# Attention with an MLP between: seven score runs per 16 key blocks, and the value sums read out by VectorE

## The chip, the cores and the metric

The kernel runs on one core of a Trainium2 chip. The metric is the device time of one execution in microseconds (us), the median over several runs; less is better. The core has a matrix engine (TensorE, "PE" in the profile, its weight loads "PEld"), VectorE ("DVE"), ScalarE ("ACT"), GpSimd ("POOL") and SyncE ("SP"), which here only issues DMA transfers. Each engine works through its own queue in order; semaphores make one engine wait for another.

## The reference

Attention and an MLP are computed from the same normalised input and added to the input (S = 2048 tokens, D = 640, 32 heads of 20, F = 1536):

```python
xn = layernorm(x)
qkv = (xn @ wqkv).reshape(B, S, 3, 32, 20).transpose(2, 0, 3, 1, 4)
p = softmax((q @ k.T) * 20 ** -0.5)
a = (p @ v).transpose(0, 2, 1, 3).reshape(B, S, 640) @ wo
y = layernorm(xn)
m = gelu(y @ w1 + b1, approximate=True) @ w2 + b2
out = x + a + m
```

## The kernel before

A first stage (up to about 232 us) normalises the input and computes queries, keys and values, and splits the weights into pairs of f16 numbers. The stage that the change touches is the attention loop, from there to about 1306 us. After it comes the rest of the projection by `wo` and the output.

**The attention loop.** The heads go in 16 pairs g, the queries in halves hf of 1024 tokens and quarters cc of 512; the keys in NKB = 16 blocks kb of 128. `ORDER` lists the pairs and halves. For each (g, hf, cc), that is 64 times, the 16 key blocks are gone through; the text calls one such pass a period.

- `scores` (L578): for one key block, four entries on TensorE (two weight loads and two matmuls, one for each head of the pair) write a tile `s` of two PSUM banks, from a pool of three such tiles (`psS`). ScalarE takes the exp of it into an SBUF tile `p` (128 x 1024, L586), from a pool `pt`.
- `rest` (L593): for half of the key blocks (`SPLIT`: the first two of each four) VectorE computes `low`, what the upper 16 bits of each p leave over, in f16 (L598). There are four such buffers.
- `pv` (L603): the products with the values for four key blocks, 16 matmul calls on 32-column parts of the array (eight with the upper halves, four with `low`, four in f32), summed in one PSUM bank `o`, whose pool `psO` has one buffer. The bank collects all 16 blocks of a period. After the last four, ScalarE copies it into `ev` (L636), one half of a tile that holds two periods; when both halves are there, `unload` (L642) writes them to DRAM with two transfers to `lpart` (the sums of p) and four to `opart`, on SP's queue, or on ScalarE's for the last entry of `ORDER`.
- `finish` (L666): when some head pairs are complete, their sums are loaded again, checked, inverted, spread over the rows, and multiplied in by VectorE (L725 to L731), step by step.

**The MLP between.** `mlp` (L829) is a generator over chunks of 256 tokens. For each chunk there are six tiles of `layer1` (30 matmuls `pu` of 256 columns in one PSUM bank) and four of `layer2` for the chunk before (36 matmuls `py` of 320 columns). They share one PSUM bank, `psM`. It yields an estimated cost in us after three `pu` or two `py` matmuls. When a `layer1` tile ends, `gelu` (L735) is begun: its VectorE operations (L740, L741; then L744, L745), a tanh on ScalarE (L748), and three more on VectorE (L750 to L752). A `yield` in it means that it goes on at the next `tick`; `tick()` moves every such side job on by one step. The end of a `layer2` tile is one VectorE operation (L757). `load_chunk` (L769) loads a chunk's input and its row of factors `r2f`.

**The order written out by hand** is the loop at L933. For every four key blocks: scores of two blocks; a tick; `rest` of the first block; a part of the MLP; scores of two blocks; a tick; `rest` of the others; and `pv` of the four blocks before. The MLP part takes steps while the credit, which grows by `rate` = 1.235 for each four blocks, is above zero, up to `CHUNK` = 1.75 in one part, and stops where a tile ends (`over`). So a period has eight score runs, four MLP parts and four value runs on TensorE.

Of the kernel before, what the change touches and what calls it, by code (L numbers as in the profile page):

```python
# [7 lines left out]
F32 = mybir.dt.float32  # L8
# [8 lines left out]
P = 128  # L17
# [15 lines left out]
CHUNK = 1.75  # L33
# [9 lines left out]
def mha_mlp_kernel(tc, x, wqkv, wo, w1, b1, w2, b2, out):  # L43
# [4 lines left out]
    with (  # L48
# [463 lines left out]
        with ExitStack() as scope:  # L512
# [4 lines left out]
            ptp = pool(name="pt", bufs=2 * GRP - 1)  # L517
# [83 lines left out]
            evs = {}  # L601

            def pv(units):  # L603
# [29 lines left out]
                if last:  # L633
                    if cc == 0:
                        evs[g, hf] = m1.tile([P, 2, 512], F32, tag="ev", name="ev")
                    nc.scalar.activation(evs[g, hf][:, cc], pv.o, AF.Copy)  # L636
                    if cc == 1:
                        unload(g, hf, evs.pop((g, hf)))
# [5 lines left out]
            def unload(g, hf, ev):  # L644
                cols = slice(hf * 1024, (hf + 1) * 1024)
                for p in range(2):
                    dma(g, hf)(lpart[p, hf, 2 * g : 2 * g + 2, :].rearrange("a (c t) -> a c t", c=2),
                                      ev[PAD + DH + VW * p :: 64])
                    for a in range(2):
                        q0, r = 64 * a + PAD + VW * p, (2 * g + a) * DH  # L650
                        dma(g, hf)(opart[p, r : r + DH, cols].rearrange("d (c t) -> d c t", c=2),
                                          ev[q0 : q0 + DH])
# [82 lines left out]
            def gelu(ps, r2f, hT, f):  # L735
# [11 lines left out]
                yield  # L747
# [18 lines left out]
            xs, hTs = {}, {}  # L766
            over = [False]

            def load_chunk(mc):  # L769
                t0 = mc * MC  # L770
                xnt = m2.tile([P, KD, 2, MC], F16, tag="xnt", name="xm")
                r2f = m2.tile([P, MC], F32, tag="r2f", name="r2f")
                nc.sync.dma_start(xnt, xscr[:, :, :, t0 : t0 + MC])
                nc.sync.dma_start(r2f, rscr[None, t0 : t0 + MC].to_broadcast([P, MC]))
                xs[mc] = xnt, r2f

            def layer1(mc, f):
                xnt, r2f = xs[mc]
# [3 lines left out]
                for i in range(2):  # L782
                    n = 0
                    fo_ = (f + i) % 4 * P
                    for k in range(KD):
                        for a, b in PASS:
                            nc.tensor.matmul(ps[:, i], w1v[:, k, (f + i) // 4, a, fo_ : fo_ + P], xnt[:, k, b, :],  # L787
                                             start=(n == 0), stop=(n == 3 * KD - 1))
                            n += 1
                            if n % 3 == 0:  # L790
                                if i == 1 and n == 15:
                                    begin(gelu(ps, r2f, hTs[mc], f))
# [36 lines left out]
            def mlp():  # L829
                load_chunk(0)  # L830
                load_chunk(1)
# [95 lines left out]
            with tc.manual_schedule():  # L927
                fill = chain()
                credit = 0.0 - next(fill)
                rate = 1.235  # L930
                groups = [(g, hf, cc, kb) for g, hf in ORDER for cc in range(2) for kb in range(0, NKB, GRP)]
                prev = None
                for g, hf, cc, kb0 in groups:  # L933
                    units = []
                    for kb in range(kb0, kb0 + GRP):
                        units.append([g, hf, cc, kb, scores(g, hf, cc, kb)])
                        if kb % 2 == 0:
                            continue
                        tick()
                        if kb % GRP == 1:  # L940

                            rest(units[0])
                            credit += rate
                            spent, over[0] = 0.0, False
                            while credit > 0 and spent < CHUNK and not over[0]:
                                cost = next(fill)
                                if cost is None:
                                    credit = 0.0  # L950
                                    break
                                credit -= cost
                                spent += cost
                        else:
                            for u in units[1:]:
                                rest(u)
                            if prev:
                                pv(prev)
                    prev = units
                    if cc == 0 and kb0 == 0 and (g, hf) != ORDER[-1]:  # L960
                        n = ORDER[ORDER.index((g, hf)) + 1]
                        sides.append(load_stack(*n, *([stacks[g, hf][1]] if n[0] == g else [])))
# [15 lines left out]
                pv(prev)  # L978
# [104 lines left out]
```

## Time and profile before

| | us |
|---|---|
| median of 3 runs | 1384.39 (1383.7 to 1385.21) |
| the profiled execution | 1385.2 |
| its span from first to last instruction | 1383.5 |
| TensorE busy | 1350.8 (98% of the span) |
| ScalarE busy | 1126.2 (81%) |
| VectorE busy | 1061.7 (77%) |

Busy times are sums over the whole span, and the stages have different limits, so the attention loop is looked at by itself. A row of the groups gives the line, the engine, the operation, the tile written and the tiles read, the count, then busy time and mean duration (ns), then the engine's idle time just before with what ended it. A row of the waits gives who waited for whom, the total in us, how often, and the longest. A row of the timeline gives the start in us from the span's start, the time that a merged group took, the engine, the line and the operation, the count, and in brackets the idle time before it with what ended it. A row of a source line gives the count, then shortest, median and longest duration in ns, and the first and last start. PE busy time counts matmuls that wait in the array too, so starts of following runs tell more than durations.

### The profile page before, as it was taken

The numbers are of one execution on the slowest core, as the hardware profiler recorded it, in microseconds if no ns is written. First come the engines' busy times: TensorE is split into PE (matmuls) and PEld (weight loads), VectorE is DVE, ScalarE is ACT, GpSimd is POOL, SyncE is SP. The second block draws the span as 40 slices with busy tenths as digits, with TensorE's granted clock in tenths as the row PEclk, the third lists the DMA queues.
The fourth block names the chain that finished last, engine by engine and source line by source line (L and its number), as shares of the span: only waits on it lengthen the run. The fifth ranks groups of instructions, "written<-read, shape, count | busy, mean of one in ns | idle before, by whom it ended". The sixth has DMA issues, their size and how long they took to land.

```text
span 1383.5 us, 29113 instructions
## 1 busy us (share of the span) xinstructions
PE 1350.8 (98%) x11711; PEld 600.9 (43%) x11711; DVE 1061.7 (77%) x1425; ACT 1126.2 (81%) x1282; POOL 32.9 (2%) x75
## 2 busy tenths in 40 slices
PE   9999999999999999999999999999999999999998
PEld 6555555443333343433343333343334334333375
DVE  6648743899778977889887789877988897888642
ACT  5644323999999999999999999999999999999700
POOL 2000000000000000000000000000000000000000
PEclk9999999999999999999999999999999999999999
DMA  9853413012124231213221123212124322341375
GB/s 265 243 175 109 108 52 110 16 32 64 41 55 111 67 88 34 69 52 102 71 77 33 47 75 103 76 47 58 44 64 113 98 56 70 85 153 59 98 235 179
DMA packets 92320, 125.68 MB, mean 91 GB/s; under 512 B 16905, under 2 KB 58569, under 8 KB 92178
## 3 DMA queue, kind: packets, MB, share of 16 engines
q1 hardware_dynamic: 89218, 117.14, 28.3%
q0 software_dynamic: 2304, 5.24, 2.3%
q8 instruction: 94, 1.54, 0.5%
q10 hardware_dynamic: 656, 1.36, 0.3%
q14 instruction: 48, 0.39, 0.1%
HBM read 80.84 MB, written 42.86 MB: 89 GB/s over the span
## 4 chain that ended last, share of the span: by engine, by line
PE 59%; DVE 11%; ACT 5%; DMA 3%; issue 2%; SPq 1%; DVEq 0%; ACTq 0%
PE o L615 23%; PE s L584 14%; PE py L819 9%; PE pu L787 8%; DVE low L598 5%; PE z L896 5%; ACT p L586 4%; DMA oscr<-oa 1%; DVE u L740 1%; DMA oa<-opart 1%; DVE u L741 1%; DVE w L744 1%; DVE w L745 1%; DVE hT L752 1%; DVE u L750 1%
## 5 line engine op out<-in xcount | busy, mean ns | idle before, releaser
L586 ACT ACTIVATE p<-s 128x1024 f32<-128x1024 f32 x1024 | 973.6, 1042 | 52.4 <-PE s L584 46.2
L598 DVE TENSOR_TENSOR low<-p 128x1024 f16<-128x1024 f32 x512 | 608.8, 1219 | 165.0 <-ACT p L586 164.9
L615 PE MATMUL o<-p,vfull 128*32 128x512 bf16 (+1 forms) x4096 | 433.7, 494 | 0.0
L584 PE MATMUL s<-qs,ks 61*128 61x512 f16 x2048 | 317.7, 382 | 8.7 <-ACT p L586 7.2
L584 PEld LDWEIGHTS <-ks 61*128 61x128 f16 x2048 | 63.9, 94 | 296.4 <-issue 294.2
L787 PE MATMUL pu<-xm,w1t 128*128 128x256 f16 x1440 | 179.2, 274 | 4.1 <-DVE u L740 3.6
L819 PE MATMUL py<-w2t,hT 128*128 128x320 f16 x1152 | 178.6, 301 | 1.7 <-DVE xb L757 1.7
L787 PEld LDWEIGHTS <-w1t 128*128 128x128 f16 x1440 | 130.9, 98 | 71.2 <-issue 57.6
L819 PEld LDWEIGHTS <-hT 128*128 128x128 f16 x1152 | 102.5, 98 | 89.5 <-issue 55.2
L286 PE MATMUL qkp<-xnt,wv 128*128 128x512 f16 x600 | 132.3, 380 | 0.0
L615 PEld LDWEIGHTS <-vfull 128*32 128x32 f16 x3072 | 61.5, 95 | 146.2 <-issue 115.4
L615 PE MATMUL o<-low,vfull 128*32 128x512 f16 x1024 | 107.3, 379 | 6.6 <-DVE low L598 6.4
L300 ACT ACTIVATE qkhl<-qkp,qks 128x1024 f16<-128x1024 f32 (+1 forms) x24 | 23.3, 971 | 84.1 <-PE qkp L286 66.2
L286 PEld LDWEIGHTS <-wv 128*128 128x128 f16 x600 | 58.2, 98 | 67.8
L615 PEld LDWEIGHTS o<-p,vfull 128*32 128x32 f32 x2048 | 63.1, 109 | 50.6 <-issue 0.5
L349 PE MATMUL vp<-wv,xnt 128*128 128x320 f16 x480 | 66.6, 300 | 0.0
L896 PE MATMUL z<-w1t,ot 128*128 128x320 f16 x480 | 65.8, 300 | 0.0
L896 PEld LDWEIGHTS <-ot 128*128 128x128 f16 x480 | 46.7, 98 | 19.8 <-issue 1.7
L349 PEld LDWEIGHTS <-xnt 128*128 128x128 f16 x480 | 46.5, 98 | 18.2
L301 DVE SCALAR_TENSOR_TENSOR qkhl<-qkp,qks,qkhl 128x1024 f16<-128x1024 f32 (+1 forms) x24 | 26.5, 1104 | 34.3 <-ACT qkhl L300 34.3
L857 DVE SCALAR_TENSOR_TENSOR acc<-z,sc,acc 128x320 f32<-128x320 f32 x32 | 17.6, 550 | 45.1 <-PE z L896 42.9
L636 ACT ACTIVATE ev<-o 128x512 f32<-128x512 f32 x64 | 39.4, 615 | 3.3 <-PE o L615 3.3
(168 smaller groups left out, 685.7 us busy)
## 6 DMA issues: line engine op xcount, KB each, us to landing
qkscr<-qkhl SPq DMA_DIRECT2D x40, 256.0 KB
opart<-ev SPq DMA_DIRECT2D x124, 80.0 KB
ks<-qkscr SPq DMA_DIRECT2D x120, 80.0 KB
qs<-qkscr SPq DMA_DIRECT2D x192, 40.0 KB
oa<-opart SPq DMA_DIRECT2D x32, 240.0 KB
xt<-in_A_x_dram SPq DMA_DIRECT2D x16, 320.0 KB
xscr<-xnt SPq DMA_DIRECT2D x4, 1280.0 KB
xm<-xscr SPq DMA_DIRECT2D x8, 640.0 KB
```

The source lines that it names most:

```text
L286: nc.tensor.matmul(ps[:, i, :], wv[:, k, q, a, mm * P : (mm + 1) * P], xnts[c][:, k, b, :], start=(k + n == 0), stop=(k == KD - 1 and n == 2))
L300: nc.scalar.activation(hl[:, 0, i0:i1], ps[:, i0:i1], AF.Copy, scale=a)
L301: nc.vector.scalar_tensor_tensor(hl[:, 1, i0:i1], ps[:, i0:i1], a, hl[:, 0, i0:i1], ALU.mult, ALU.subtract)
L349: nc.tensor.matmul(ps[:, hf, :320], xnts[c][:, k, a, j * P : (j + 1) * P], wv[:, k, 2, b, hf * 320 : (hf + 1) * 320], start=(n == 0), stop ...
L584: nc.tensor.matmul(ps[:, a, :], ks[64 * a : 64 * a + 61, kb * P : (kb + 1) * P], qs[64 * a : 64 * a + 61, cc * 512 : (cc + 1) * 512], star ...
L586: nc.scalar.activation(pt, ps, AF.Exp, scale=QS)
L598: nc.vector.tensor_sub(low, pt, upper(pt))
L615: nc.tensor.matmul(pv.o[32 * q : 32 * q + 32, :], src[:, v0 - PAD * (1 - q % 2) :][:, :32], t, start=q not in pv.begun, stop=last, skip_gr ...
L636: nc.scalar.activation(evs[g, hf][:, cc], pv.o, AF.Copy)
L787: nc.tensor.matmul(ps[:, i], w1v[:, k, (f + i) // 4, a, fo_ : fo_ + P], xnt[:, k, b, :], start=(n == 0), stop=(n == 3 * KD - 1))
L819: nc.tensor.matmul(ps[:, :320], hTs[mc][:, f, a, j * P : (j + 1) * P], w2v[:, f, b, hf * 320 : (hf + 1) * 320], start=(n == 0), stop=(n == ...
L896: nc.tensor.matmul(ps[:, :320], ot[:, k, a, j * P : (j + 1) * P], wov[:, k, b, h * 320 : (h + 1) * 320], start=(n == 0), stop=(n == 3 * KD ...
```

## The change

The order of a period is written anew. Scores run in seven runs, up to blocks 3, 5, 7, 9, 12, 14 and 16. After each there is a tick, then `rest` of all new blocks, and then one piece of other work: an MLP part after 3, 7 and 14, and the value products of the last period's blocks 12 to 15 after 5, and of this period's blocks 0 to 3, 4 to 7 and 8 to 11 after 9, 12 and 16. `rate` is 1.647 for each of the three parts (1.235 x 4 = 4.94 for a period before), `CHUNK` is 2.0. The pool of p tiles has eight buffers for seven. VectorE copies the value sums out of PSUM, into a buffer of 512 tokens (one buffer), and `unload` writes each 512 tokens at once, with the same six transfers of half the size. `gelu` has one `yield` less. The factors `r2f` have one buffer for two and are loaded by `load_factors`, when the last `layer1` tile of the chunk before has ended, ahead of `load_chunk` for the chunk after.

```diff
-CHUNK = 1.75
+CHUNK = 2.0
-            ptp = pool(name="pt", bufs=2 * GRP - 1)
+            ptp = pool(name="pt", bufs=2 * GRP)
...
                 if last:
-                    if cc == 0:
-                        evs[g, hf] = m1.tile([P, 2, 512], F32, tag="ev", name="ev")
-                    nc.scalar.activation(evs[g, hf][:, cc], pv.o, AF.Copy)
-                    if cc == 1:
-                        unload(g, hf, evs.pop((g, hf)))
+                    ev = m1.tile([P, 512], F32, tag="ev", name="ev")
+                    nc.vector.tensor_copy(ev, pv.o)
+                    unload(g, hf, cc, ev)
...
-            def unload(g, hf, ev):
-                cols = slice(hf * 1024, (hf + 1) * 1024)
+            def unload(g, hf, cc, ev):
+                c0 = cc * 512
                 for p in range(2):
-                    dma(g, hf)(lpart[p, hf, 2 * g : 2 * g + 2, :].rearrange("a (c t) -> a c t", c=2),
-                                      ev[PAD + DH + VW * p :: 64])
+                    dma(g, hf)(lpart[p, hf, 2 * g : 2 * g + 2, c0 : c0 + 512], ev[PAD + DH + VW * p :: 64])
                     for a in range(2):
                         q0, r = 64 * a + PAD + VW * p, (2 * g + a) * DH
-                        dma(g, hf)(opart[p, r : r + DH, cols].rearrange("d (c t) -> d c t", c=2),
-                                          ev[q0 : q0 + DH])
-                if g + 1 in ENDS:
+                        dma(g, hf)(opart[p, r : r + DH, hf * 1024 + c0 : hf * 1024 + c0 + 512], ev[q0 : q0 + DH])
+                if cc == 1 and g + 1 in ENDS:
...
                 nc.vector.scalar_tensor_tensor(w, w, 1.0 / 0.044715, u, ALU.add, ALU.mult)
                 yield
-                yield
                 nc.scalar.activation(w, w, AF.Tanh, scale=0.7978845608028654 * 0.044715)
...
+            def load_factors(mc):
+                r2f = m1.tile([P, MC], F32, tag="r2f", name="r2f")
+                nc.sync.dma_start(r2f, rscr[None, mc * MC : (mc + 1) * MC].to_broadcast([P, MC]))
+                fs[mc] = r2f
...
                 if f == KF - 2:
+                    if mc + 1 < NMC:
+                        load_factors(mc + 1)
                     if mc + 2 < NMC:
                         load_chunk(mc + 2)
...
-                rate = 1.235
-                groups = [(g, hf, cc, kb) for g, hf in ORDER for cc in range(2) for kb in range(0, NKB, GRP)]
...
+                rate = 1.647
+                after = {3: "mlp", 5: -GRP, 7: "mlp", 9: 0, 12: GRP, 14: "mlp", 16: 2 * GRP}
+                prev, units, new = None, [], []
+                for g, hf in ORDER:
+                    for cc in range(2):
+                        prev, units = units, []
+                        for kb in range(NKB):
+                            units.append([g, hf, cc, kb, scores(g, hf, cc, kb)])
+                            new.append(units[-1])
+                            work = after.get(kb + 1)
+                            if work is None:
+                                continue
+                            tick()
+                            for u in new:
+                                rest(u)
+                            new.clear()
+                            if work == "mlp":
+                                credit += rate
+                                spent, over[0] = 0.0, False
+                                while credit > 0 and spent < CHUNK and not over[0]:
+                                    cost = next(fill)
...
+                            elif work >= 0:
+                                pv(units[work : work + GRP])
+                                units[work : work + GRP] = [None] * GRP
+                            elif prev:
+                                pv(prev[work:])
+                                prev = None
+                                del u
+                            if cc == 0 and work == -GRP and (g, hf) != ORDER[-1]:
+                                n = ORDER[ORDER.index((g, hf)) + 1]
+                                sides.append(load_stack(*n, *([stacks[g, hf][1]] if n[0] == g else [])))
```

More of the change, by code (lines that the diff above doesn't have):

```diff
@@ L791, in layer1 @@
                                 if i == 1 and n == 15:
-                                    begin(gelu(ps, r2f, hTs[mc], f))
+                                    begin(gelu(ps, fs[mc], hTs[mc], f))
                                     over[0] = True
@@ L929, in mha_mlp_kernel @@
                 credit = 0.0 - next(fill)
-                rate = 1.235
-                groups = [(g, hf, cc, kb) for g, hf in ORDER for cc in range(2) for kb in range(0, NKB, GRP)]
[L932 to L955, printed above, removed]
-                                rest(u)
[L957 to L962, printed above, removed]
```

17 lines of the change are left out of this document (10 added, 7 removed).

## The prediction

> **What bounds the kernel now.** I read the page's first and fourth parts, then the busy time of the stage with the attention loop (253 to 1309 us), then TensorE's waits in it, then the timeline of single groups. The page, and the windows' row (busy us and instructions of PE, PEld, DVE, ACT, POOL, then clock, DMA):
>
> ```profile
> span 1383.5 us, 29113 instructions
> PE 59%; DVE 11%; ACT 5%; DMA 3%; issue 2%; SPq 1%; DVEq 0%; ACTq 0%
> 253.00:1309.00 1056.00, 1036.06 (x9618) 413.67 (x9618) 887.23 (x1058) 1002.65 (x1126) 15.92 (x18) 1.00 0.25 69
> PE o L615 <- DVE low L598: 6.4, 11, 1.5
> PE s L584 <- ACT p L586: 5.7, 21, 0.5
> PE pu L787 <- DVE u L740: 3.6, 4, 2.0
> PE py L819 <- DVE xb L757: 1.7, 2, 1.3
> ```
>
> TensorE is busy 98% of the stage, ScalarE 95%, VectorE 84%; the chain of waits is mostly TensorE's. TensorE waits little, and not mainly for ScalarE. What one period (16 key blocks, 512 tokens) takes is the distance between two read-outs of the value sums: the source's row gives the first start, the timeline's the 63rd.
>
> ```profile
> L636 ACT ACTIVATE ev<-o x64: 597/601/750, 253.6 to 1309.7; 128x512 f32<-128x512 f32 x64
> 1295.36 0.60 ACT L636 ACTIVATE ev<-o 128x512 f32<-128x512 f32 x1
> ```
>
> (1295.36 - 253.6) / 62 = 16.80 us. Of this TensorE's own work, from starts in the timeline:
>
> ```profile
> 565.56 2.14 PE L787 MATMUL pu<-xm,w1t 128*128 128x256 f16 x18
> 567.63 0.61 PE L584 MATMUL s<-qs,ks 61*128 61x512 f16 x4
> 568.17 0.64 PE L615 MATMUL o<-p,vfull 128*32 128x512 bf16 x8
> 569.81 0.60 PE L584 MATMUL s<-qs,ks 61*128 61x512 f16 x4
> 570.35 1.49 PE L787 MATMUL pu<-xm,w1t 128*128 128x256 f16 x12
> 571.76 0.61 PE L584 MATMUL s<-qs,ks 61*128 61x512 f16 x4
> 1295.76 1.26 PE L819 MATMUL py<-w2t,hT 128*128 128x320 f16 x8
> 1296.95 0.60 PE L584 MATMUL s<-qs,ks 61*128 61x512 f16 x4
> 1299.66 1.53 PE L819 MATMUL py<-w2t,hT 128*128 128x320 f16 x10
> 1301.13 0.60 PE L584 MATMUL s<-qs,ks 61*128 61x512 f16 x4
> ```
>
> A score run of two blocks costs 0.53, a value run (PV) 1.64, 12 and 18 pu matmuls 1.41 and 2.07 (0.11 each and 0.1 a part), 8 and 10 py 1.19 and 1.47 (0.14 each and 0.1 a part). The 1440 pu and 1152 py are 157 + 158 = 315 us, 4.93 a period. So before: 8 x 0.53 + 4 x 1.64 + 4.93 + 4 x 0.10 = 16.13, and 0.67 a period (43 us in 64) is lost in waits, those above and slower matmuls around them.
>
> **The change, part by part.** TensorE: five score runs of two and two of three, and three MLP parts. A third block adds 0.22 (four matmuls record 0.61, two 0.39, below): 0.75. So 5 x 0.53 + 2 x 0.75 + 4 x 1.64 + 4.93 + 3 x 0.10 = 15.94, 0.19 less, 12 us in all. That is the certain gain. What follows can eat it.
>
> *Uneven MLP parts.* A part ends at a tile's end or when its cost passes CHUNK = 2.0. A pu tile of 30 is cut 21 + 9 and a py tile of 36 is cut 16 + 16 + 4: 2.40, 1.09, 2.29, 2.29, 0.64 us. One round of a chunk (six pu, four py tiles) has 24 parts, eight periods exactly, so the places repeat. Call the places A (behind blocks 0-2), B (behind 5, 6), C (behind 12, 13). By the code A/B/C hold 9/21/9, 16/16/4, 21/9/16, 16/4/21, 9/16/16, 4/21/9, 16/16/4, 21/9/21. How fast ScalarE gives score banks back:
>
> ```profile
> 561.54 0.61 PE L584 MATMUL s<-qs,ks 61*128 61x512 f16 x4
> 561.97 5.61 ACT L586 ACTIVATE p<-s 128x1024 f32<-128x1024 f32 x6 [0.19 <-PE s L584]
> 562.46 0.39 PE L584 MATMUL s<-qs,ks 61*128 61x512 f16 x2
> 563.05 0.39 PE L584 MATMUL s<-qs,ks 61*128 61x512 f16 x2 [0.20 <-ACT p L586]
> L586 ACT ACTIVATE p<-s 128x1024 f32<-128x1024 f32 x1024 | 973.6, 1042 | 52.4 <-PE s L584 46.2
> ```
>
> The first exp starts 0.43 after the scores, the next ones every (5.61 - 1.04) / 5 = 0.91, and there are three banks: the fourth block goes 1.51 after the first, the fifth 2.42. Blocks 0-2 start a period (T0) with ScalarE idle. Block 4 then goes at T0 + 2.42; TensorE is there at 0.75 + A + 0.22. It waits 1.45 - A: 0.36 where A is 9, 0.81 where it is 4. Likewise blocks 9-11 (T9) find ScalarE idle, since exp 8 needs a p tile that PV 0-3 frees; the bank of exp 15 comes back at T9 + 1.51 + 6 x 0.91 = 6.97, and TensorE wants it for the next block 2 at 0.75 + 1.64 + 0.53 + C + 0.53 + 1.64 + 0.44 = 5.53 + C: 0.35 for 9, 0.80 for 4. With B = 4 about 0.1. Over a round: A 0.36 x 2 + 0.81, C 0.35 x 2 + 0.80 x 2, B 0.1, together 3.93, or **0.49 a period**.
>
> *The read-out on VectorE.* The sums have one bank; the next product (PV 0-3) waits for the copy. VectorE takes it behind what its queue holds:
>
> ```profile
> 563.03 1.23 DVE L598 TENSOR_TENSOR low<-p 128x1024 f16<-128x1024 f32 x1 [1.62 <-ACT p L586]
> 564.17 0.55 DVE L757 SCALAR_TENSOR_TENSOR xb<-py,sc,xb 128x320 f32<-128x320 f32 x1
> 572.46 0.69 DVE L740 TENSOR_TENSOR u<-pu,r2f 128x512 f32<-128x512 f32 x1
> 575.25 3.49 DVE L598 TENSOR_TENSOR low<-p 128x1024 f16<-128x1024 f32 x3
> 578.89 0.69 DVE L750 SCALAR_TENSOR_TENSOR u<-w,u 128x512 f32<-128x512 f32 x1 [0.15 <-ACT w L748]
> 580.81 2.35 DVE L598 TENSOR_TENSOR low<-p 128x1024 f16<-128x1024 f32 x2
> L729 DVE CAST oa<-oa 120x512 f16<-120x512 f32 x16 | 6.7, 421 | 0.0
> L740 DVE TENSOR_TENSOR u<-pu,r2f 128x512 f32<-128x512 f32 x48 | 32.9, 685 | 0.8
> ```
>
> A low takes 1.14, the first half of a gelu (four operations) 2.79, its end (three) 1.92. No row shows the copy: 0.42 (L729, from SBUF) to 0.69 (L740, which reads these banks); I take 0.65, nearest L740. With a gelu tile ending in A, the queue is low 0, low 1, four gelu operations, low 4, copy: 1.51 + 2 x 1.14 + 2.79 + 1.14 + 0.65 + 0.04 = T0 + 8.41. TensorE reaches PV 0-3 (9/21) at 0.75 + 1.09 + 0.36 + 0.53 + 1.64 + 0.53 + 2.40 + 0.53 = 7.83: waits 0.58; 0.69 with 9/16. With one ending in the C before, low 0 starts only at 3.13 (low 12 at T9 + 4.24, low 13, four gelu operations), and low 0, low 1, the gelu's end, low 4 and the copy end at 9.16 against 8.91: 0.25, in two periods of eight. With B = 4 the copy (7.3) is 0.3 late. Else it is in time. Sum 2.07 a round, **0.26 a period**. The copy's own wait, for PV 12-15, ends before low 4 does; behind it stands low 5, wanted only by PV 4-7. Before, ScalarE copied between two exps, with two score runs and an MLP part until the next product.
>
> [...]
>
> *What stays of the 0.67.* The longest single waits are in dense VectorE stretches: gelus back to back, and the finishing of whole heads, whose rows stand in the same queue.
>
> ```profile
> 454.08 1.47 PE L787 MATMUL pu<-xm,w1t 128*128 128x256 f16 x12 [1.99 <-DVE u L740]
> L725 DVE TENSOR_TENSOR oa<-oa 120x512 f32<-120x512 f32 x16 | 11.0, 686 | 2.7 <-DMA rb<-linv 1.5 <-DMA oa<-opart 1.2
> 575.23 0.79 SPq L651 DMA_DIRECT2D opart<-ev  x2
> 1310.31 1.08 ACTq L647 DMA_DIRECT2D lpart<-ev  x1
> L651 ACTq DMA_DIRECT2D opart<-ev x4: 279/341/420, 1311.4 to 1313.3; - x4
> ```
>
> For the lows the change gives room: from a product's last low to the product lay 1.64 + 0.53 + 1.33 + 0.53 = 4.0 us of other runs, and now 4.4 (low 9, PV 8-11) to 7.0. But VectorE takes on 0.65 a period, and such work ahead of a copy makes it later still (0.69 for each finishing row). Carried over: between 0 and 0.67; I take 0.30, a little under half, for the one against the other.
>
> *The rest.* ScalarE loses 0.60 a period; it idles that much more, since neither A, C nor the copy waits for its total. The unload is issued for each 512 tokens: 32 more times two lpart and four opart DMAs, at about 0.4 on SP (L651) some 80 us of SP's time over the stage; behind them on SP stand query, chunk and factor loads that are wanted a period or more later, and ev, one buffer now, is wanted again 16 us later: nothing, and only if SP fell a whole period behind would VectorE stand at the copy. The factor load, now in one buffer and moved ahead of the chunk's, waits on SP for the gelu's first operation, a few us, and is wanted two parts later: nothing. Eight p tiles for seven, and the yield taken out of the gelu against fewer ticks: inside the schedule above. One place costs: the last query half unloads through ScalarE's queue, and its first 512 tokens now do so in mid-loop. ScalarE waits there for the copy (exp 4 ends near 5, the copy 7.3 at the earliest) and then issues six DMAs, 1310.3 to 1313.6 = 3.3 us, with exp 5 behind them: exp 5 starts near 10.6 instead of 5, block 8 wants its bank back at 7.5 and gets it at 11.7. 4.2 us, once. After the loop the tail is the same projection on TensorE.
>
> **Sum.** 15.94 + 0.49 + 0.26 + 0.30 = 16.99 against 16.80, x 64 = +12; + 4 = +16. The profiled execution took 1385.2 (its span 1383.5 and 1.7 around it), 0.8 over the median of the runs, 1384.39. So 1385 + 16 = 1401.
>
> **Rivals.** *The waits don't come* (faster). The read-out leaves ScalarE, the parts are fewer, and the copy is in time: for it speaks that the lows get room and that ScalarE is 95% busy; against it, that VectorE's queue is in order and block 4 can't go before T0 + 2.42. With half of the new waits and of the carry, 15.94 + 0.38 + 0.15 = 16.47: -21 + 4, 1368. It decides from where new waits and carry stay under 0.79 a period. [...]
>
> *VectorE's queue decides* (slower by more). The finishing and the dense gelus strike the copy as hard as they struck the lows: the whole 0.67 stays, 17.36, +36 + 4 = 1425. For it: VectorE goes from 84% to about 87% of a tightly coupled stage. Against it: the half of the periods without a gelu ahead of the copy has room for a finishing row.
>
> *Nothing to measure.* The 0.19 and the carry that vanishes pay for the new waits: 16.69 + 0.05 = 16.74, 1385.
>
> **How the numbers follow.** The forecast's case 0.50, the stronger one 0.18, no new waits 0.27, nothing to measure 0.05; 0.2% (2.8 us) is about what a measurement of this kernel can tell. The range's upper end is the carry's bound, 1425. Below: no carry (16.69) and a copy of 0.42 (five waits shorter by 0.23 a round, 0.14 a period) gives 16.55: -16 + 4, 1373; as the case without the waits has its middle at 1368 and more chance than may be left out, I put 1364, and 1426 above. The forecast's own range is 1388 to 1415.
>
> **What would show it.** Right: TensorE's waits list scores for exp near 0.49 x 64 = 31 us, and a new row, value products for the copy, near 17 us; periods between read-outs near 17 us; ScalarE's busy share of the stage down from 95% to about 90; a stretch of 3 us of DMA issue on ScalarE in the last period. The row of lows (6.4) shrinks. Wrong: if the copy's wait is under 5 us, VectorE runs ahead of my queue; if the scores' wait stays below 15, ScalarE gains ground before blocks 0 and 9 where I start it idle.

## The result, and the profile after

The changed kernel takes **1426.11 us** (median; 1425.09 to 1426.52) against 1385.21 us (1383.7 to 1385.77) for the kernel before: a ratio of 1.029, 95% interval 1.028 to 1.030. It is 41 us slower. The direction was forecast, the size was not: 1401 was put down, 16 us more than before, and the range ended at 1426.

The page of the changed kernel: its span, the shares of the chain of waits that ended last, and its groups for the value products and the read-out (line, engine, operation, tiles, count, busy us and mean ns, then the idle time before with its cause):

```profile
span 1424.4 us, 29501 instructions
PE 58%; DVE 16%; ACT 11%; DMA 6%; issue 6%; SPq 2%; ACTq 0%; DVEq 0%; POOL 0%
L613 PE MATMUL o<-p,vfull 128*32 128x512 bf16 (+1 forms) x4096 | 430.8, 495 | 30.0 <-DVE ev L633 29.2
L633 DVE COPY ev<-o 128x512 f32<-128x512 f32 x64 | 43.7, 683 | 3.5 <-PE o L613 3.5
```

VectorE and ScalarE have more of the chain than before (11% and 5% there). The value products, which before waited for `low`, now wait for the copy (`ev`). The copy takes 683 ns.

TensorE's waits in the whole span (total us, times, longest):

```profile
PE s L584 <- ACT p L586: 29.2, 76, 7.3
PE o L613 <- DVE ev L633: 29.2, 34, 1.5
```

Now the stages. The marks are the first copy of the sums, the 61st and the 64th, so the first window is 60 periods. First the changed kernel, then the one before (the window and its length, then busy us of PE, PEld, DVE, ACT, POOL with the number of instructions, then TensorE's granted clock as a share of its full speed, the DMA share and GB/s):

```profile
258.50:1282.50 1024.00, 975.35 (x9151) 414.88 (x9151) 877.87 (x1043) 929.55 (x1007) 13.14 (x15) 1.00 0.25 67
1282.50:1343.50 61.00, 49.10 (x418) 18.46 (x416) 43.53 (x74) 43.19 (x53) 2.37 (x3) 0.89 0.23 68
1343.50:1424.40 80.90, 71.68 (x529) 51.56 (x527) 24.52 (x47) 0.00 (x0) 0.00 (x0) 0.95 0.65 199
```

```profile
253.60:1258.80 1005.20, 988.36 (x9184) 395.56 (x9183) 844.26 (x987) 958.83 (x1080) 13.11 (x15) 1.00 0.25 70
1258.80:1309.70 50.90, 47.80 (x432) 18.05 (x433) 42.40 (x70) 43.23 (x50) 2.81 (x3) 1.00 0.20 56
1309.70:1383.50 73.80, 67.05 (x507) 48.51 (x505) 23.39 (x45) 0.58 (x1) 0.00 (x0) 0.98 0.69 212
```

So the 40.9 us by which the spans differ are: 4.9 to the first copy (253.6 to 258.5), **18.9 in the 60 periods** (16.75 to 17.07 each), **10.0 in the last three**, **7.1 behind the last copy**. A little under half of the loss is in the loop's steady run, where all of the forecast's terms but one lie; 22 us are at its two ends, where the forecast had 4. In the last two windows the granted clock is 0.89 and 0.95, where the kernel before has 1.00 and 0.98.

One period, with a `gelu` ahead of the copy. T0 is 729.11, when block 0's scores start (start us, duration, engine, line, operation; in brackets the idle time before and what ended it):

```profile
729.11 0.82 PE L584 MATMUL s<-qs,ks 61*128 61x512 f16 x6
729.86 1.16 PE L783 MATMUL pu<-xm,w1t 128*128 128x256 f16 x9
730.60 2.36 DVE L598 TENSOR_TENSOR low<-p 128x1024 f16<-128x1024 f32 x2 [0.38 <-ACT p L586]
730.95 0.39 PE L584 MATMUL s<-qs,ks 61*128 61x512 f16 x2
731.53 0.39 PE L584 MATMUL s<-qs,ks 61*128 61x512 f16 x2 [0.19 <-ACT p L586]
732.88 0.34 DVE L733 TENSOR_SCALAR r2f<-r2f,sc 128x256 f32<-128x256 f32 x1
733.33 0.69 DVE L734 TENSOR_TENSOR u<-pu,r2f 128x512 f32<-128x512 f32 x1
...
735.50 0.69 DVE L739 SCALAR_TENSOR_TENSOR w<-w,u 128x512 f32<-128x512 f32 x1
736.11 1.22 DVE L598 TENSOR_TENSOR low<-p 128x1024 f16<-128x1024 f32 x1
737.25 0.68 DVE L633 COPY ev<-o 128x512 f32<-128x512 f32 x1
737.98 0.64 PE L613 MATMUL o<-p,vfull 128*32 128x512 bf16 x8 [0.92 <-DVE ev L633]
```

The order in VectorE's queue is the forecast one: two lows, the gelu, a low, the copy. Block 4's scores start at T0 + 2.42. Two score matmuls are 0.22 of work, and 0.58 lies between the starts at 730.95 and 731.53: 0.36 is lost, of which the view lists 0.19. The same holds for all 66 waits of scores for exp in the 60 periods: from the starts of the matmuls just before to the starts of those that waited it is 40.9 us in sum, of which 66 x 0.22 = 14.5 is work, so 26.4 are lost where the list has 15.7. The value products start at T0 + 8.87.

The last query half, where ScalarE's queue issues the six transfers in mid-loop:

```profile
1314.83 0.82 PE L584 MATMUL s<-qs,ks 61*128 61x512 f16 x6
...
1323.85 0.68 DVE L633 COPY ev<-o 128x512 f32<-128x512 f32 x1
1324.56 1.08 ACTq L643 DMA_DIRECT2D lpart<-ev  x1
...
1326.97 0.80 ACTq L646 DMA_DIRECT2D opart<-ev  x2
1327.87 3.77 ACT L586 ACTIVATE p<-s 128x1024 f32<-128x1024 f32 x4 [7.58 <-DMA opart<-ev]
1328.95 0.61 PE L584 MATMUL s<-qs,ks 61*128 61x512 f16 x2 [7.33 <-ACT p L586]
1330.75 1.92 PE L613 MATMUL o<-p,vfull 128*32 128x512 f32 x8
1332.60 1.46 PE L584 MATMUL s<-qs,ks 61*128 61x512 f16 x6
...
1335.09 1.03 PE L613 MATMUL o<-p,vfull 128*32 128x512 f32 x8
```

T0 is 1314.83 here; the copy ends at T0 + 9.70. TensorE stands for 7.33 us, and the matmuls behind that run slow (1.92 for 1.03, 1.46 for 0.82) until 1335. Earlier in the last three periods there is another wait: ScalarE stands at the load of `wo`, which the kernel before does not, and the scores behind it wait 2.83 us.

```profile
1288.43 0.74 ACT L541 ACTIVATE junk<-w1t 128x640 bf16<-128x640 f32 x1 [3.13 <-DMA w1t<-in_A_wo_dram]
```

And the tail (`z` are the projection's matmuls, `rb` those that spread the inverted sums over the rows), first of the changed kernel, then of the one before:

```profile
1343.34 2.35 PE L817 MATMUL py<-w2t,hT 128*128 128x320 f16 x16
1345.52 9.13 PE L895 MATMUL z<-w1t,ot 128*128 128x320 f16 x66
1356.95 2.90 PE L710 MATMUL rb<-lt,sel 64*80 64x64 f32 x32 [2.30 <-DVE lt L701]
```

```profile
1309.54 12.40 PE L896 MATMUL z<-w1t,ot 128*128 128x320 f16 x90
1321.87 2.50 PE L716 MATMUL rb<-lt,sel 64*80 64x64 f32 x32
```

The rest of the MLP, which the loop had not taken (16 py), runs behind the last value products, and of the projection 66 matmuls instead of 90 stand ahead of `rb` to cover the load and inversion of the last sums: `rb` waits 2.30.

### The profile page after: what moved, and what is told of

Same layout as the page of the kernel before. It is cut to its first block, busy times and chain, and to the rows that moved or that the text cites. A ratio compares the mean times of both kernels' runs of the same rounds, so it can differ in the third digit from the quotient of the medians.

```text
span 1424.4 us, 29501 instructions
## 1 busy us (share of the span) xinstructions
PE 1347.4 (95%) x11711; PEld 625.6 (44%) x11711; DVE 1101.8 (77%) x1489; ACT 1100.1 (77%) x1218; POOL 32.5 (2%) x75
## 3 DMA queue, kind: packets, MB, share of 16 engines
q8 instruction: 94, 1.54, 0.5%
## 4 chain that ended last, share of the span: by engine, by line
PE 58%; DVE 16%; ACT 11%; DMA 6%; issue 6%; SPq 2%; ACTq 0%; DVEq 0%; POOL 0%
PE o L613 17%; ACT p L586 11%; PE s L584 11%; DVE low L598 8%; PE qkp L286 7%; PE pu L783 7%; PE py L817 6%; PE vp L349 4%; PE z L895 4%; DVE ev L633 2%; DMA qkscr<-qkhl 1%; DMA ks<-qkscr 1%; DMA w1t<-in_A_wo_dram 1%; DVE u L734 1%; DVE w L738 1%
## 5 line engine op out<-in xcount | busy, mean ns | idle before, releaser
L586 ACT ACTIVATE p<-s 128x1024 f32<-128x1024 f32 x1024 | 969.6, 1041 | 102.2 <-PE s L584 78.1
L613 PE MATMUL o<-p,vfull 128*32 128x512 bf16 (+1 forms) x4096 | 430.8, 495 | 30.0 <-DVE ev L633 29.2
L584 PE MATMUL s<-qs,ks 61*128 61x512 f16 x2048 | 315.9, 383 | 29.9 <-ACT p L586 29.2
L584 PEld LDWEIGHTS <-ks 61*128 61x128 f16 x2048 | 79.0, 94 | 333.4 <-issue 314.7
L783 PE MATMUL pu<-xm,w1t 128*128 128x256 f16 x1440 | 175.2, 274 | 3.0 <-DVE u L734 3.0
L817 PE MATMUL py<-w2t,hT 128*128 128x320 f16 x1152 | 174.2, 301 | 0.0
L783 PEld LDWEIGHTS <-w1t 128*128 128x128 f16 x1440 | 133.8, 98 | 53.7 <-issue 39.0
L613 PE MATMUL o<-low,vfull 128*32 128x512 f16 x1024 | 100.8, 379 | 0.0
L613 PEld LDWEIGHTS o<-p,vfull 128*32 128x32 f32 x2048 | 63.1, 109 | 54.9 <-issue 1.3
L301 DVE SCALAR_TENSOR_TENSOR qkhl<-qkp,qks,qkhl 128x1024 f16<-128x1024 f32 (+1 forms) x24 | 26.5, 1104 | 36.1 <-ACT qkhl L300 36.1
L633 DVE COPY ev<-o 128x512 f32<-128x512 f32 x64 | 43.7, 683 | 3.5 <-PE o L613 3.5
```

What stands on the lines that cost most here:

```text
L301: nc.vector.scalar_tensor_tensor(hl[:, 1, i0:i1], ps[:, i0:i1], a, hl[:, 0, i0:i1], ALU.mult, ALU.subtract)
L584: nc.tensor.matmul(ps[:, a, :], ks[64 * a : 64 * a + 61, kb * P : (kb + 1) * P], qs[64 * a : 64 * a + 61, cc * 512 : (cc + 1) * 512], star ...
L586: nc.scalar.activation(pt, ps, AF.Exp, scale=QS)
L613: nc.tensor.matmul(pv.o[32 * q : 32 * q + 32, :], src[:, v0 - PAD * (1 - q % 2) :][:, :32], t, start=q not in pv.begun, stop=last, skip_gr ...
L633: nc.vector.tensor_copy(ev, pv.o)
L817: nc.tensor.matmul(ps[:, :320], hTs[mc][:, f, a, j * P : (j + 1) * P], w2v[:, f, b, hf * 320 : (hf + 1) * 320], start=(n == 0), stop=(n == ...
```

## The experiments

All edits are to the changed kernel unless said; none leaves any work out. Ratios are to runs of the kernel before on the same chip. This table, from the starts of the copies in each profiled execution, is what the readings rest on (us): the start of the first scores, from there to the first copy, the mean of the next 60 periods, the last three together, and from the last copy to the end. The start of the first scores differs by some us between executions whose first stage is the same code; no reading rests on it. The time to the first copy is not exact either: it is 26.1 in the changed kernel and 24.8 in g2, which has the same code up to there.

| | first scores | to first copy | period | last three | tail | median |
|---|---|---|---|---|---|---|
| before | 232.5 | 21.1 | 16.753 | 50.9 | 73.8 | 1385.2 |
| after | 232.4 | 26.1 | 17.068 | 61.0 | 80.9 | 1426.1 |
| e1 copy on ScalarE | 231.2 | 21.7 | 16.689 | 56.4 | 76.9 | 1391.9 |
| e2 even parts | 232.5 | 24.7 | 16.974 | 59.2 | 78.1 | 1414.6 |
| e3 unload on SP | 233.0 | 26.0 | 17.071 | 54.7 | 85.4 | 1425.3 |
| e4 copy first | 234.0 | 22.6 | 16.743 | 65.6 | 82.6 | 1411.1 |
| e5 = e1 + e2 | 232.5 | 21.9 | 16.261 | 57.2 | 77.5 | 1366.1 |
| e6 = e4 + e2 | 236.2 | 22.1 | 16.345 | 65.4 | 77.8 | 1379.8 |
| e7 e3, credit, early load | 233.2 | 28.7 | 17.131 | 53.3 | 74.0 | 1418.6 |
| e8 before, copy on VectorE | 238.2 | 22.9 | 16.810 | 53.1 | 75.1 | 1397.4 |
| f1 = e5 + e7 | 240.8 | 26.3 | 16.347 | 51.5 | 74.1 | 1366.4 |
| f2 = e6 + e7 | 231.9 | 26.5 | 16.669 | 50.4 | 74.1 | 1388.7 |
| g1 credit alone | 232.9 | 29.0 | 17.131 | 54.9 | 74.0 | 1420.8 |
| g2 early load alone | 231.4 | 24.8 | 17.073 | 61.7 | 81.2 | 1427.7 |

My theory was that of the prediction: VectorE's queue in front of the copy, and uneven MLP parts, cost the periods their gain, and the mid-loop unload costs a few us once. The rivals: that the copy itself is to blame wherever it stands in VectorE's queue, and that the ends of the loop cost for other reasons.

**e1: the read-out back on ScalarE, in the new order.**

```diff
-                    nc.vector.tensor_copy(ev, pv.o)
+                    nc.scalar.activation(ev, pv.o, AF.Copy)
```

> The changed kernel with one line put back: ScalarE copies the value sums out of PSUM, all else as changed. If the copy's place in VectorE's queue costs what the trace shows (29.2 us of TensorE's waits for it), those waits fall under 5 us; ScalarE has 0.60 us a period more and the waits of scores for exp grow by some us. In the last query half ScalarE no longer waits for VectorE before it issues the DMAs. Time 1397 to 1408. Rival, the copy's wait only covers work that is late anyway (ScalarE's exps, the MLP's uneven parts): the waits of scores take its place and the time stays at 1420 or more.

1391.86 us, ratio 1.0035 (1.002 to 1.0051): 34 of the 41 us are gone, more than expected. The wait for the copy has left the list of TensorE's waits; that of the scores remains, a little smaller and not grown as expected:

```profile
PE s L584 <- ACT p L586: 25.3, 81, 3.6
```

**e2: even MLP parts.** With 1.5 a pu tile is cut 15 + 15 and a py tile 12 + 12 + 12.

```diff
-CHUNK = 2.0
+CHUNK = 1.5
```

> The changed kernel with CHUNK 1.5 for 2.0: the MLP tiles are cut 15 + 15 and 12 + 12 + 12 instead of 21 + 9 and 16 + 16 + 4, in the same number of parts, so that the gelus end at the same places. If uneven parts cause the waits of scores for exp (15.7 us in the 60 full periods), these fall under 4 us. Value products after 7 come sooner in the periods where a 21 or 16 stood there, so the waits for the copy grow from 29 to about 34 us (0.9 us in two periods of eight, 1.2 in two more). Together 1414 to 1421. Rival, the parts decide alone and the copy does not matter: below 1410. Rival, they do not matter: 1425 or more, with the waits of scores unchanged.

1414.6 us, 1.021 (1.017 to 1.025), as expected. The scores' wait falls from 29.2 to 12.7 us, but the copy's rises from 29.2 to 43.2: what no longer waits for ScalarE arrives at the copy earlier. Alone it gains 0.09 a period.

**e5: both.**

> Both at once: ScalarE copies the value sums (as in e1_copy_scalar) and the MLP tiles are cut evenly (CHUNK 1.5, as in e2_even_parts). If e1_copy_scalar's remaining 25.3 us of scores waiting for exp come from the uneven parts, they fall under 10 us (what is left being the edge places near the end) and the period from 16.69 to about 16.4: 1372 to 1382, below the kernel before. Rival, ScalarE with the copy is itself the limit (exps, copy and tanh near 95% of the stage): the waits stay above 18 us and the time at 1387 or more.

**1366.1 us, 0.986 (0.984 to 0.988)**, below the expectation, and faster than the kernel before. The period falls to 16.26, which is less than by the two apart: with the copy on ScalarE the even parts are worth 0.43 a period, not 0.09. Its 60 periods by the windows:

```profile
254.40:1230.00 975.60, 968.55 (x9162) 410.32 (x9162) 846.32 (x985) 949.91 (x1069) 13.11 (x15) 1.00 0.26 70
```

And TensorE's wait for exp in its whole span, 29.2 in the changed kernel:

```profile
PE s L584 <- ACT p L586: 11.3, 16, 3.2
```

ScalarE is busy 949.91 of 975.60, 97%, and only f1, below, which takes the same time, comes as high (97% from its first copy to the 61st); these two are the fastest kernels here.

**e4: the copy stays on VectorE, but first in its queue.** The last value products are issued ahead of the tick and of the lows.

```diff
+                            if work == -GRP and prev:
+                                pv(prev[work:])
+                                prev = None
                             tick()
                             for u in new:
                                 rest(u)
                             new.clear()
...
-                            elif prev:
-                                pv(prev[work:])
-                                prev = None
```

> The changed kernel with the order at one place turned: after block 5 the value products of the last period and the copy are issued ahead of the tick and of low 4, so the copy stands in front of the gelu's operations and of low 4 in VectorE's queue, which then waits for the products' end instead. Same instructions, same engines. If the place in the queue is the cause and not VectorE's total work, the waits for the copy fall from 29 to under 8 us and the time to 1400 to 1412. Rival, VectorE is simply too full: what is behind the copy comes late instead (value products for low, MLP for the gelu's first operation) and the time stays above 1420.

1411.1 us, 1.0175 (1.014 to 1.021). The period is 16.74, that of before, and no value product waits for the copy; VectorE now waits for the products instead (38.5 us, without harm). So it was the place in the queue, not the engine. What stands behind the copy pays a little: the MLP's waits for the gelu's first operation are 7.2 us, 3.0 in the changed kernel. At the end of the loop 4.6 us of the gain are lost again: there the scores wait 7.0 once. TensorE's longest wait, and from the view of line 633 what VectorE's copy waited for:

```profile
PE s L584 <- ACT p L586: 32.6, 75, 7.0
```

```profile
  PE o L613: 38.5, 37
```

**e6: copy first and even parts.**

> The copy in front of the gelu and of low 4 in VectorE's queue (as in e4_copy_first) with evenly cut parts. The waits of scores for exp (32.6 us in e4_copy_first, 7 of them at one place near the end) fall to about 15 us, the period from 16.74 to about 16.4: 1390 to 1400, the edges near the end staying as they are. Rival, VectorE's total work is the limit: the MLP's waits for the gelu's first operation grow over 10 us and the time stays at 1405 or more.

1379.76 us, 0.995 (0.993 to 0.997), better than expected: the read-out on VectorE, mended at both places, is a little faster than the kernel before.

**e8: the kernel before, with the copy on VectorE and nothing else.**

```diff
-                    nc.scalar.activation(evs[g, hf][:, cc], pv.o, AF.Copy)
+                    nc.vector.tensor_copy(evs[g, hf][:, cc], pv.o)
```

> The kernel before with one line changed: VectorE copies the value sums out, in the order before (eight score runs, four MLP parts). If the copy costs only where it stands behind a gelu and low 4, with the next product one read-out later, it costs little here, where only low 1 stands between: waits for the copy under 8 us, ScalarE relieved by 0.6 us a period without use: 1383 to 1392. Rival, VectorE's total work decides wherever the copy stands: 20 us of new waits or more, 1403 or more.

1397.42 us, 1.0077 (1.0056 to 1.0098): neither expectation. The waits for the copy are 12.6 us, expected were under 8. In the periods the move costs 0.057 each, 3.4 us in 60, where it costs 0.38 each, 22.7 us, in the new order (e1 to after); so it is the new order that makes the move dear. The ends take 5 us, and the first scores start 5.7 us later in this execution, which the edit doesn't touch; how much of that is in the median isn't settled.

**e3: the mid-loop unload on SP's queue.**

```diff
-                return (nc.scalar if (g, hf) == ORDER[-1] else nc.sync).dma_start
+                return (nc.scalar if (g, hf) == ORDER[-1] and cc == 1 else nc.sync).dma_start
```

> The changed kernel, but the first 512 tokens of the last query half go out by SP's queue, like all before them; ScalarE's queue only unloads the last 512. If the 7.3 us wait of scores near the end comes from the DMA issue in ScalarE's queue behind the copy, it goes, and with it the slow matmuls behind it (granted clock 0.89 in that stretch): 8 to 11 us less, 1415 to 1418. Rival, another engine is late there too (the output weights' preparation on VectorE): 2 us less or nothing.

1425.28 us, 1.027 (1.024 to 1.031): nothing gained, so the theory of a cost that simply goes away fell. The last three periods lose 6.3 us, and the tail takes 4.5 of them back, 1.5 in a longer wait at `rb`; the projection that should cover the last sums' load has not grown. Most of the rest is the clock: behind that wait TensorE's granted clock is 0.50 for about 10 us (1352.5 to 1362.7), in the changed kernel for 3.4 (1358.8 to 1362.2), so some 3 us of work more are lost: the 32 `rb` take 4.50 us here and 2.90 there, and the z behind them 0.161 each (111 in 17.87) and 0.140 (366 in 51.07).

```profile
PE rb L710 <- DVE lt L701: 3.8, 1, 3.8
```

**e7: e3, and the credit starting a part higher, and the load of `wo` issued four steps earlier.**

```diff
-                credit = 0.0 - next(fill)
+                credit = 2.0 - next(fill)
...
-                                               range(KD), 4))
+                                               range(KD), 8))
```

> The changed kernel with its period as it is and three things at the edges: the first 512 tokens of the last query half unload through SP's queue (as in e3_sync_unload), the MLP's credit starts at 0 instead of -2.0, so that no MLP part is left for the tail, and the preparation of the output weights waits 8 ticks instead of 4 behind the issue of their load. If the edges cost what the two traces' difference says (10 us in the last three periods, 7 in the tail), ScalarE no longer stands at that load, the selection matmuls in the tail no longer wait (2.3 us), and TensorE's granted clock in the last periods rises from 0.89 to 0.97 or more: 1408 to 1416. Rival, as in e3_sync_unload, the loss only moves into the tail: 1420 or more.

1418.58 us, 1.024 (1.022 to 1.026), 2.6 above the expectation. The last three periods and the tail lose 14.6 us together, but the first copy comes 2.7 later and the period grows by 0.06. To tell the three edits apart, two were run alone.

**g1: the credit alone.**

> The changed kernel with the credit starting at 0 instead of -2.0, alone. The loop then takes the MLP part that was left over behind it (2.35 us of py at the tail's start). Theory: the places at which gelus fall do not matter much, the tail falls from 80.9 to 76 to 78, the first copy comes 2 to 3 us later, the period stays within 0.07 of 17.07: 1422 to 1428 us, nothing to measure or a little slower. Rival: the leftover part is what makes the tail long (through the wait behind it and the slow matmuls after that wait): tail 73 to 75, 1417 to 1421 us.

1420.76 us, 1.0245 (1.023 to 1.026), the rival's time. The last three periods lose 6.0 us and the tail 6.9, to 74.0, with before's rows again (90 z, no wait at `rb`):

```profile
1332.35 0.39 PE L584 MATMUL s<-qs,ks 61*128 61x512 f16 x2 [3.89 <-ACT p L586]
...
1344.54 12.40 PE L895 MATMUL z<-w1t,ot 128*128 128x320 f16 x90
1356.87 2.50 PE L710 MATMUL rb<-lt,sel 64*80 64x64 f32 x32
```

So the tail's 7 us come from what was left over of the MLP. The mid-loop unload is still on ScalarE here and costs less (3.89 for 7.33). The gain is partly paid at the other end: the first copy 2.9 later, and 0.06 a period, 3.8 us, as other tiles end in other places.

**g2: the earlier load alone.**

> The changed kernel with the `wo` load issued four steps ahead of what it was (delay 8), alone. Theory: ScalarE's wait for the `wo` load (3.1 us) and the wait of the scores behind it (2.83 us) go, with the slower matmuls after them: the last three intervals fall from 60.96 to 56 to 58, the tail stays at 80.9: 1421 to 1424 us. Rival: the wait only moves to the next thing in the same queue (the long opart wait 35 us later absorbs it, since that place waits on VectorE's copy): under 1 us, 1425 to 1427 us.

1427.72 us, 1.029 (1.028 to 1.031): nothing gained. That is the rival's time, and its reading in part: the wait only moves. ScalarE no longer stands at the load of `wo`, but at nearly the same place the scores now wait 2.36 us for their keys, whose transfer SP issues at 1291.49, behind the six transfers of an unload:

```profile
1293.12 1.09 PE L584 MATMUL s<-qs,ks 61*128 61x512 f16 x5 [2.36 <-DMA ks<-bscr]
```

The wait at the mid-loop unload is 4.94 for 7.33 here, and the last three periods still take 61.7; where the difference goes was not told apart.

**f1 and f2: the three edits of e7 on the two mended versions.**

> Three edits at the two ends of the loop, on top of the copy on ScalarE with CHUNK 1.5 (1366.1 us): only the very last 512 tokens unload through ScalarE's queue, the credit starts at 0 instead of -2.0 so that the loop takes the last MLP part, and the `wo` load is issued four steps ahead of what it was. Theory (the ends cost time of their own, and in this version not hidden by anything): the period stays at 16.26 us; ScalarE's wait for the `wo` load (3.6 us) and its six transfers in mid-loop go, the leftover part no longer delays the tail: the last three intervals fall from 57.2 to about 53, the tail from 77.5 to about 74, the first copy comes 2 to 3 us later (an MLP part more before it): 1359 to 1363 us. Rival (a gain at one end is given back at the other, as where SP unloaded alone): the sum of last intervals and tail stays within 2 us of 134.7, and the time is 1366 to 1369 us, later by the first part.

> The same three edits on top of the copy ahead of the tick on VectorE with CHUNK 1.5 (1379.76 us). Theory: the period stays near 16.35 us; the last three intervals, 65.4 there with a ScalarE wait of 9.2 us for the `wo` load, fall to 54 to 57, the tail from 77.8 to about 75: 1367 to 1373 us. It would show that the read-out by VectorE with its place and the parts mended is faster than before too, by about 1%. Rival: the long wait in the last intervals is that of the scores for an exp which stands behind the copy's transfers on ScalarE and has another cause than these; then 1376 us and more.

f1: 1366.35 us, 0.985 (0.984 to 0.987), the same as e5. The last three periods and the tail lose 9.1 us, not kept within 2 as the rival had it, but the first copy comes 4.4 later and the periods take 0.09 each, 5.2 us: nothing is left. (Its profiled execution took 1375.3, with a first stage 8 us longer.) f2: 1388.69 us, 1.002 (1.0004 to 1.0034), far above the expectation: 18.7 us are gained behind the 61st copy, more than it had, 4.4 lost ahead of the first, and 19.4 lost in the periods (16.345 to 16.669), which none of the edits was meant to touch. The credit moves every tile's end to another place; here twelve of the 60 periods are 18 us or longer, in e6 three. Of the waits in its 60 periods the scores' on exp grows from 3.6 (e6) to 10.2, and waits of scores on a DMA (4.8) and of py on a gelu (from 1.5 to 4.4) come with it. Which of them sets it off was not told apart.

## Why the prediction was right and wrong

**The step that failed** is the one on the ends: "One place costs: the last query half unloads through ScalarE's queue … 4.2 us, once. After the loop the tail is the same projection on TensorE." Forecast were 4 us; measured, from the copies' starts, 4.9 + 10.0 + 7.1 = 22. That is 18 of the 25 us by which the forecast of +16 missed the +41; the other 7 are in the periods, where the term for what stays of the old waits was too small.

- The tail is not the same. The MLP has 192 parts (48 pu tiles of two, 32 py tiles of three), and the loop now has 3 x 64 = 192 places for them, where it had 256. The credit starts at -2.0 and a place adds 1.647, so the first place takes nothing, and the low credit cuts a tile near the start once more (12 + 15 + 3). So two parts, 4 and 16 py, are left when the loop ends; the 16 run behind the last value products, and 24 projection matmuls fewer stand there to cover the last sums' load. g1 starts the credit at 0, and the tail is 74.0 (before 73.8). That cost could have been counted from the code.
- The mid-loop unload was found, and its chain (copy, six transfers, exps, scores) is in the rows; but it held TensorE for 7.33 us, not 4.2: the copy ended at T0 + 9.70, not at the earliest place of 7.3, with finishing and weight preparation in VectorE's queue beside it, and slow matmuls followed. e3 shows that without it the last three periods are 6.3 us shorter; in g1, where other parts fall in those places, it holds TensorE for 3.89. The scores' wait of 2.83 us behind the load of `wo`, with 1.1 us of slower matmuls after it, was in no term; g2 shows that taking the load's lateness away alone gains nothing. As the tail took most of e3's gain back, the costs of the end are not ones to add up singly.
- Of the 4.9 to the first copy, 4.4 go when ScalarE copies (e1: 21.7 for 26.1). Not all of that is the queue: TensorE's granted clock up to the first copy is 0.87 in the changed kernel and 0.92 in e1 (and in the kernel before), and g2 with the queue unchanged has 24.8.

**The period was nearly right**: 16.99 forecast, 17.07 measured over the 60 periods. As a loss it was less so: 0.19 a period was forecast, from 16.80, and 0.315 is measured, since before these 60 periods take 16.75; 0.125 x 60 = 7.5 us. By its terms:

- *Uneven parts, 0.49.* T0 + 2.42 for block 4 and a wait of 0.36 stand in the timeline to the hundredth. The waits list shows 15.7 us in 60 periods against the forecast's 29 or so, because it understates each wait; by the starts it is 26.4, or 0.44 a period. By experiment the term is 0.43 (e1 to e5) or 0.40 (e4 to e6). Nearly right, a little too large.
- *The read-out behind VectorE's queue, 0.26.* The mechanism is right and the row is there, but 29.0 us are listed in 60 periods, 0.48 each, and taking it away is worth 0.33 (e4), 0.38 (e1), and with even parts 0.63 and 0.71. The queue itself was sized well. In the period shown the products went at T0 + 8.87 for 8.41, and nearly all of that is L733 (0.34, and 0.45 from its start to the next), which comes once in a chunk and had been left out; the four gelu operations take 2.78 from start to start for 2.79, and the copy 0.683 for 0.65. Where no finishing row stands near the copy, the products of a round wait 0.61, 0.92, 0.27 and twice 0.13, together 2.06 for the forecast's 2.07.
- *What stays of the 0.67, taken as 0.30.* This is the term of the period that was too small. The other waits for the copy come in the first chunk, where gelus stand back to back (4.8 us for the first five copies), and above all where rows of the finishing stand ahead of the copy in VectorE's queue, which the forecast had counted here. At the same places of a round they make 1.08 of 0.61, 1.40 of 0.92 and 0.95 or 1.54 of 0.13; one of them, with a finishing row ahead of low 0:

```profile
697.55 0.68 DVE L725 TENSOR_TENSOR oa<-oa 120x512 f16<-120x512 f32 x1
704.20 0.64 PE L613 MATMUL o<-p,vfull 128*32 128x512 bf16 x8 [0.95 <-DVE ev L633]
```

  17.07 less 15.94, the 0.44 and the 0.26 leaves 0.43 for what was put at 0.30, a choice between two bounds. e5, without uneven parts and without a copy on VectorE, leaves 0.32 (16.26), and e6, with the copy first in the queue, 0.40 (16.35).

The terms don't add up as the forecast let them, either: mended alone the two new ones give 0.09 or 0.38, together 0.81 (e5) or 0.72 (e6). e2 shows how: the scores wait less, and the copy is waited for 14 us more.

So the stronger rival's time, 1425, came true by luck, without its mechanism: it put the whole 0.67 into each period, 17.36, and the period is 17.07. Its finishing rows and dense gelus in front of the copy were in part what happened; their size was not.

**The other signs.** ScalarE's share of the stage fell from 95% to 929.55 / 1024.0 = 91%, as forecast (about 90). The row of lows has gone from the list. The stretch of DMA issue on ScalarE is there, 1324.56 to 1327.87, 3.3 us. Taking the copies off ScalarE, which was busy 95% of the stage before, cost 34 us in the new order (1391.9 in e1, 1426.1 in the changed kernel), and the fastest kernel has ScalarE at 97%. e4 shows that the waits were for a place in an ordered queue, not for capacity: with the same instructions on the same engines and the copy ahead in the queue, the period is 16.74 for 17.07.

## What to carry to other kernels

Where sums have one bank, the instruction that reads them out is on the path (29.2 us of TensorE's waits here): look at what stands in front of it in its engine's queue at that moment, not at how busy the engine is, and put it first (e4: a period of 16.74 for 17.07) or in a queue where less stands in front of it (e1: 16.69). When a written order gets fewer and larger places for filling work, count the places against the parts, and walk the first and last period by themselves: here more than half of the loss was there. And terms that wait on neighbouring points of one queue are to be mended together and measured together: alone, the even parts showed 0.09 of their 0.43, and the copy about half (0.38 of 0.71).

## What the runs showed of the hardware

After some stops of TensorE, not after all, the next matmuls ran slower for some microseconds. After 7.33 us the eight f32 value matmuls took 1.92 for 1.03 and six scores 1.46 for 0.82. After 2.83 us sixteen py took 3.45 for 2.35:

```profile
1290.22 0.39 PE L584 MATMUL s<-qs,ks 61*128 61x512 f16 x2 [2.83 <-ACT p L586]
1291.68 3.45 PE L817 MATMUL py<-w2t,hT 128*128 128x320 f16 x16
```

In g1, after a wait of 1.91 us, they took 2.33, where another sixteen in that run took 2.35. The granted clock goes with it: it is 0.50 from 1324.7 to 1334.9 and 0.51 from 1290.5 to 1294.0, and 1.00 between. The length of the stop does not decide alone. In e7 and in g1 the value products wait 2.62 us for the copy at the same place of the same code; first e7, with a granted clock of 1.00 from 448.5 to 455.0 and the eight f32 products in 1.05, then g1, with 0.74 and 1.96, where the first row is the same:

```profile
448.46 0.64 PE L613 MATMUL o<-p,vfull 128*32 128x512 bf16 x8 [2.62 <-DVE ev L633]
449.13 1.05 PE L613 MATMUL o<-p,vfull 128*32 128x512 f32 x8
```

```profile
449.24 1.96 PE L613 MATMUL o<-p,vfull 128*32 128x512 f32 x8
```

So a single wait can cost more than its length, and the same wait need not in another run: behind the stop of 2.83 us 1.1 us more were lost in slow matmuls, and behind one of 2.62 us the value products ran slow in g1 and not in e7.

The other surprise is of the trace: of a wait between two short matmuls the view listed 0.19 where the starts show 0.36 lost. Over the 66 waits of the 60 periods 15.7 us are listed and 26.4 are lost, so some 11 us stand in no row of the list.
